# Second half of the adaLN modulation: from matmuls in the first phase to multiply-adds on GpSimd in units 8 to 11

## The chip, the cores and the metric

The kernel runs on one core of a Trainium2 chip. The metric is the device time of one execution in microseconds (us). Three runs of the kernel before took 1102.35, 1103.45 and 1103.99 us; their median is 1103.45 us. Engines are named as in the profile: PE is TensorE's matmul, PEld its weight load, DVE is VectorE, ACT is ScalarE, POOL is GpSimd, and SP is SyncE, which here issues nearly all DMAs. Each engine works through its own instructions in the order written; a wait of one instruction holds everything behind it on that engine.

## The reference

One transformer block over 2048 tokens of width 448, conditioned by a vector `c`: attention with 16 heads of 28, then a GELU MLP of width 1792, each behind a layer norm that is scaled, shifted and gated by six vectors of 448.

```python
mod = (silu(c) @ w_mod).reshape(1, 6, 1, -1)          # c: 1x448, w_mod: 448x2688
sa, ca, ga, sb, cb, gb = (mod[:, i] for i in range(6))
h = layernorm(x) * (1 + ca) + sa
q, k, v = (h @ wqkv) ...                               # 16 heads, 28 each
x = x + ga * (softmax(q @ k.T * 28**-0.5) @ v) @ wo
h = layernorm(x) * (1 + cb) + sb
y = layernorm(h)                                       # the MLP has its own
x = x + gb * (gelu(y @ w1 + b1) @ w2 + b2)
```

All is float32. The change concerns `ga`, `sb`, `cb` and `gb` only: the second part of the modulation, columns 896 to 2687 of `w_mod`.

## The kernel before

Precision is kept by splitting each operand into a high and a low float32 part (`hi`, `lo`), so that a product is three matmuls. The program has three parts in a row.

**The first phase** works on four blocks of 512 tokens. A block `b` is a list of tasks: a Q or K projection for a group of four heads (`qk_task`), or a V projection for 128 tokens (`v_task`). A task is 11 matmuls. The softmax needs the maximum of every score row before the exponentials, and it is found by a cheaper, separate pass: a *row maximum* is one matmul of a 128x28 piece of Q with a 28x512 piece of K (`max_mm`), and a DVE reduction of the 128x512 result to one column (`max_one`). There are 1024 of these, 64 for each *unit* (a group of heads with 512 queries). After each task `emit_task` puts four or five row maxima on PE. Their PSUM banks come from a ring of five (`ps_mx`). A further bank, `o` (`ps_o`), is used for a *sixth* matmul in tasks in which nothing else needs it: the flag `p1_n[1]`. Some tasks also have four row maxima between the halves of their 11 matmuls (`emit_mid`). One matmul in most tasks belongs to a pair: ACT takes the ReLU of a difference and DVE adds the other row maximum (`pair_diff`, its `rest`).

In block 1 the bank `o` is held by the second part of the modulation. Tasks 0 to 3 of that block end with `mod_mm`: four matmuls of 32x448, the SiLU of `c` (32 equal columns) times a piece of `w_mod`, which lies in the slots `v2` and `v3`; so the flag is off for these tasks. `mod_fin` then copies the bank to SBUF on ACT, sends it to DRAM (`drow`) and loads it back four times as a row that every partition holds (`rows["ga"]` and so on).

**The second phase** has 16 units of 16 *steps*, 256 in all. A step does the scores of 128 keys with 512 queries for four heads (12 matmuls, `L1348`), two exponentials on ACT (`L1361`), and the product of the step before with V (`av`, `L1303`). What is left of the row maxima is strewn into the steps. From step 121 (`RING`) there are three a step: one in the only bank `m1`, reduced by `L481`, and two in a double bank of the score tiles, reduced together by `L686`. Steps 8 to 11 of units 13 and 14 also carry the output projection (`is_wo`). When no row maximum is left, the scores take all score tiles (`three`).

At the end of a unit, tasks with fixed steps (`unit_end_tasks`) form the softmax denominators: step 1 of the next unit sends them out over SP (`L1046`), step 4 takes reciprocals on DVE and bounces them through DRAM (`L1054`, `L1056`), step 10 multiplies on POOL (`L1061`), step 11 rounds to `hi` on DVE (`L1071`), takes `lo` on POOL (`L1072`), and stores both. Other work has its step in a table, `sched`, filled by `at(step, fn)`. In each step's list, what was entered first comes first; the entries of the unit ends are made while the program is written out, so they come after those made ahead of it. Steps 4 to 14 hold the preparation of `wo` (scaled by `ga` on POOL, rounded on DVE: `wo_item`), step 15 and 28 the load and scaling of `b2`.

**The third part** is the MLP.

Of the kernel before, what the change touches and what calls it, by code (L numbers as in the profile page):

```python
# [22 lines left out]
D = 448  # L23
# [21 lines left out]
def tile_adaln_block(ctx: ExitStack, tc: tile.TileContext, x, wqkv, wo, w1, b1, w2, b2, c, w_mod, out):  # L45
# [33 lines left out]
    def sbt(tag, shape, dt=F32, bufs=1):  # L79
        return sb.tile(shape, dt, tag=tag, name=nm(tag), bufs=bufs)  # L80
# [40 lines left out]

    ident = sbt("ident", [128, 128])
    make_identity(nc, ident)
    cst = sbt("cst", [128, 5])
    neg_half, zero_col = cst[:, 0:4], cst[:, 4:5]
    pool.memset(neg_half, -0.5)
    pool.memset(zero_col, 0.0)


    cols = sbt("cols", [128, 2 * NC])  # L130
# [607 lines left out]

    mod = {}

    def mod_load(k):
        mod[k] = slot(f"v{2 + k % 2}", [128, 4 * D], F32)
        load_mod(mod[k], k, 2 * D, 4)

    def mod_mm(k):
        if k == 0:
            mod["p"] = ps_o()
        p = mod["p"]
        for j in range(4):
            rs_, cs = mod_part(k, j, 4)  # L750
            pe.matmul(
                p[32 * j : 32 * j + 32, :D], sil_b[rs_, k, :], mod[k][rs_, cs],
                start=(k == 0), stop=(k == NC - 1),
            )

    def mod_fin():
        t = sbt("full", [128, 512], bufs=3)
        act.copy(t[0:64, :D], mod["p"][0:64, :D])
# [58 lines left out]
    for b in range(NB):  # L817
# [12 lines left out]
        for n, (tb, kind, g) in enumerate(tasks):  # L830
# [7 lines left out]
                p1_n[0] = 0  # L838

            k = n - (6, 4, 4, 4)[b]  # L840
            p1_n[1] = not (more and (0 <= k < NC)) and not (b == 1 and n < 4)
            p1_n[2] = (3 if n > 4 else 1) if b == 3 else 2 if b == 2 and p1_n[1] else 1
            p1_n[3] = emit_mid if (b, n) in ((1, 1), (1, 3), (1, 5), (1, 7), (2, 8)) else None
            p1_n[4] = not more
# [27 lines left out]
                    later[n - 7](None)  # L872
            if n == (4 if b else 6):
                v_init(b)
            if b == 0 and n == 6:
                mod_load(0)
                mod_load(1)
# [4 lines left out]
            if b == 1:  # L882
                if n < 2:
                    mod_mm(n)
                    mod_load(2 + n)
                elif n in (2, 3):
                    mod_mm(n)
                    if n == 3:
                        mod_fin()
            if not more:  # L890
                if n == 0:
                    load_q(0)
# [68 lines left out]
    def wo_item(n):  # L961
        def ld(r):
            if n == 4:
                pool.memset(r[:, :D], 0.0)
                for j in range(4):
                    sp.dma_start(r[32 * j : 32 * j + DH, :D], wo[NP + DH * j : NP + DH * j + DH, :])
                return
            p0 = 0
            for r0, r1 in (((128 * n, 128 * n + 128),), MIX_HI, MIX_LO)[max(0, n - 1)]:
                sp.dma_start(r[p0 : p0 + r1 - r0, :D], wo[r0:r1, :])  # L970
                p0 += r1 - r0

        def go(r):
            full = sbt("full", [128, 512], bufs=3)
            ps = slice(0, 112 if n == 3 else 128)
            pool.tensor_tensor(out=full[ps, :D], in0=r[ps, :D], in1=rows["ga"][ps], op=ALU.mult)

            def rest():
                if n == 3:
                    hi = sbt("hi", [128, 512], F32R, bufs=3)  # L980
                    dve.tensor_copy(hi[ps, :D], full[ps, :D])
                    pool.tensor_tensor(out=wo_p[1][ps, 2, :], in0=full[ps, :D], in1=f(hi)[ps, :D], op=ALU.subtract)
                    pool.tensor_copy(wo_p[1][0:32, 2, :], f(hi)[0:32, :D])
                    return
                k = min(n, 3)
                dve.tensor_copy(wo_p[0][:, k, :], full[:, :D])
# [3 lines left out]
            at(6 + 2 * n, rest)  # L990

        return ld, go

# [511 lines left out]
```

## Time and profile before

| | us |
|---|---|
| median of three runs | 1103.45 |
| the profiled execution | 1103.82 |
| its span | 1101.7 |
| first phase (ends with the first score matmul) | 0 to 167.1 |
| second phase, steps 0 to 255 | 167.1 to 791.1 |
| step 121 on, a step without projection | 2.1 to 2.3 |
| last units, no row maximum left | about 2.0 a step |

The times of steps are taken from the first of the twelve score matmuls of each step. A row of the timeline gives the start in us from the span's beginning, the length, the engine, the line, the operation, the tile written and those read, and in brackets the idle time of the engine before it with what ended it. The granted TensorE clock is 1.00 throughout.

### The profile page before, as it was taken

To read this page: it belongs to the slowest core of one execution; us is meant where nothing else is said; L and a number is where in the kernel's file an instruction comes from. 1 tells how busy PE (TensorE), PEld (TensorE's weight loads), DVE (VectorE), ACT (ScalarE), POOL (GpSimd) and SP (SyncE) were. 2 spreads that over 40 slices of the span, in tenths; PEclk is the share of its full clock that TensorE was granted. 3 is DMA by queue.
4 is the path that set the end of the run, shared out by engine and by line. 5 is a ranking of instruction groups with operands and counts; after the bars stand their busy time and mean duration, and the time that the engine had idled before them with its cause. 6 is when DMAs were issued, how large, how long until landed. Compare 5 with 4: busy or idle time off the path is not lost.

```text
span 1101.7 us, 20731 instructions
## 1 busy us (share of the span) xinstructions
PE 1094.3 (99%) x8303; PEld 665.3 (60%) x8303; DVE 798.9 (73%) x1382; ACT 697.3 (63%) x883; POOL 196.8 (18%) x201
## 2 busy tenths in 40 slices
PE   9999999999999999999999999999999999999998
PEld 6756675444444444444444444554488888888887
DVE  6968788999999989988888888574655644444322
ACT  4655667888888888888888888678933411211210
POOL 1543332210000000000000000116123214023000
PEclk9999999999999999999999999999999999999999
DMA  9553354221222201231211313111451000000000
GB/s 311 199 191 106 99 183 138 60 64 33 75 76 61 76 28 40 69 102 47 69 48 38 98 42 99 57 31 59 146 144 50 27 34 1 15 20 1 34 1 34
DMA packets 51094, 82.67 MB, mean 75 GB/s; under 512 B 13327, under 2 KB 19878, under 8 KB 50986
## 3 DMA queue, kind: packets, MB, share of 16 engines
q1 hardware_dynamic: 50514, 80.61, 23.9%
q8 instruction: 65, 1.06, 0.4%
q10 hardware_dynamic: 148, 0.46, 0.1%
q0 software_dynamic: 336, 0.28, 0.1%
q14 instruction: 31, 0.25, 0.1%
HBM read 56.25 MB, written 26.75 MB: 75 GB/s over the span
## 4 chain that ended last, share of the span: by engine, by line
PE 97%; DVE 1%; ACT 0%; DMA 0%; issue 0%; ACTq 0%; DVEq 0%
PE s L1348 23%; PE o L1303 23%; PE m L396 17%; PE pa L396 9%; PE m L476 8%; PE s L1439 3%; PE s L1440 3%; PE s L1438 3%; PE s L476 2%; PE t L1439 1%; PE t L1440 1%; PE t L1438 1%; PE o L277 1%; DVE mxp L481 0%; PE ma L476 0%; PE m L277 0%
## 5 line engine op out<-in xcount | busy, mean ns | idle before, releaser
L481 DVE TENSOR_REDUCE mxp<-m 128x1 f32<-128x512 f32 x555 | 359.9, 686 | 64.7 <-PE m L476 46.9
L1348 PE MATMUL s<-slot_b,slot_a 28*128 28x512 f32 (+1 forms) x3072 | 356.7, 423 | 0.0
L1348 PEld LDWEIGHTS s<-slot_b,slot_a 28*128 28x128 f32 (+1 forms) x3072 | 211.2, 183 | 175.8 <-ACT slot_c L1361 96.4
L476 PE MATMUL m<-kh,qh 28*128 28x512 f32 x607 | 227.0, 468 | 0.4 <-DVE mxp L481 0.3
L1361 ACT ACTIVATE slot_c<-s 128x1024 f32<-128x1024 f32 x170 | 174.8, 1028 | 51.5 <-PE s L1348 50.8
L1303 PE MATMUL o<-slot_c,v 128*32 128x512 f32 x680 | 178.9, 605 | 0.0
L1394 ACT ACTIVATE full<-m,b_col 128x512 f32<-128x512 f32 x56 | 38.6, 689 | 205.3 <-PE m L396 188.5
L686 DVE TENSOR_REDUCE mxp<-s 128x2 f32<-128x1024 f32 x107 | 131.2, 1226 | 5.0
L1303 PE MATMUL o<-slot_c1h,v 128*32 128x512 f32 x512 | 134.7, 605 | 0.0
L1303 PE MATMUL o<-slot_c0h,v 128*32 128x512 f32 x508 | 133.6, 605 | 0.0
L1361 ACT ACTIVATE slot_c1h<-s 128x1024 f32<-128x1024 f32 x128 | 130.7, 1021 | 0.0
L1361 ACT ACTIVATE slot_c0h<-s 128x1024 f32<-128x1024 f32 x127 | 130.5, 1027 | 0.0
L1397 DVE CAST hi<-full 128x512 fp32r<-128x512 f32 x42 | 18.6, 443 | 121.1 <-ACT full L1394 121.1
L1361 ACT ACTIVATE slot_d<-s 128x1024 f32<-128x1024 f32 x86 | 88.4, 1028 | 25.2 <-PE s L1348 24.9
L476 PEld LDWEIGHTS m<-kh,qh 28*128 28x128 f32 x607 | 90.8, 182 | 15.2 <-DVE mxp L481 13.3
L1303 PE MATMUL o<-slot_d,v 128*32 128x512 f32 x344 | 90.5, 605 | 0.4 <-ACT osb L1267 0.4
L1061 POOL TENSOR_TENSOR osb<-osb,osb 128x512 f32<-128x512 f32 x16 | 20.6, 1284 | 363.5 <-DMA osb<-drec 247.1
L1398 DVE TENSOR_TENSOR lo<-full,hi 128x512 fp32r<-128x512 f32 x56 | 43.0, 768 | 26.6 <-ACT hi L1397 22.6
L396 PE MATMUL m<-y,slot_a 128*128 128x512 f32 x160 | 60.7, 395 | 0.0
L481 DVE TENSOR_REDUCE mxp<-ma 128x1 f32<-128x512 f32 x61 | 39.5, 682 | 13.2 <-PE m L476 8.0
L1303 PEld LDWEIGHTS o<-slot_c,v 128*32 128x32 f32 x680 | 24.5, 108 | 39.0 <-issue 36.4
L650 DVE CUSTOM_DVE_ANT_0 slot_d0i<-m,slot_d0i 128x512 f32<-128x512 f32 x54 | 37.3, 691 | 14.3 <-PE m L476 11.6
(351 smaller groups left out, 1835.7 us busy)
## 6 DMA issues: line engine op xcount, KB each, us to landing
slot_b<-d SPq DMA_DIRECT2D x32, 256.0 KB
slot_a<-d SPq DMA_DIRECT2D x32, 256.0 KB
d<-lo SPq DMA_DIRECT2D x28, 256.0 KB
d<-hi SPq DMA_DIRECT2D x16, 256.0 KB
osb<-drec SPq DMA_DIRECT2D x15, 256.0 KB
out_dram<-xn SPq DMA_DIRECT2D x16, 224.0 KB
raw<-in_B_w_dram SPq DMA_DIRECT2D x14, 224.0 KB
qh<-d SPq DMA_DIRECT2D x12, 256.0 KB
```

Source lines behind the costliest of these rows:

```text
L396: pe.matmul(p, a, b, start=(i == 0), stop=(i == len(terms) - 1))
L476: pe.matmul(m, qh_sb[(g, qt)][js, i * 128 : (i + 1) * 128], k[js, :], start=True, stop=True)
L481: dve.tensor_reduce(out=mxp[(g, qt)][:, i, j, cch : cch + 1], in_=m, op=ALU.max, axis=AX.X)
L686: dve.tensor_reduce(out=mxp[(g, qt)][:, i, j : j + 2, cch], in_=t, op=ALU.max, axis=AX.X)
L1303: pe.matmul(o[32 * j : 32 * j + 32, :], v_sb[kt // 4][:, kt % 4, 4 * g + j, :], p[j // 2][:, j % 2, :], start=(kt == 0), stop=(kt == NKT - 1),
L1348: pe.matmul(s2[:, jj, :], ks[rows_, kp, kc], qs[rows_, qp, :], start=(term == 0), stop=(term == 2))
L1361: act.activation(pt[hf], s2, AF.Exp, scale=SCALE)
L1394: act.activation(gf, p, AF.Gelu_apprx_tanh, bias=b1_col[:, i : i + 1])
L1398: dve.tensor_tensor(out=glo, in0=gf, in1=f(ghi), op=ALU.subtract)
L1438: pe.matmul(pp, ghi[:, ts], w_hi, start=(m == 0), stop=False)
L1439: pe.matmul(pp, ghi[:, ts], w_lo, start=False, stop=False)
L1440: pe.matmul(pp, glo[:, ts], w_hi, start=False, stop=(m == NFT - 1))
```

## The change

The second part of the modulation is no longer a matmul. `mod_load` brings a half of a row block of `w_mod` (128x896, 448 KB; the last block has 64 rows) into the one slot `a2h`; `mod_add` multiplies it on POOL by the SiLU column of `c` and adds it to a running sum in `b1h` (for `ga`, `sb`) or `a3h` (for `cb`, `gb`). There are eight such pairs of load and multiply-add, one every three steps from step 130 (`MOD_AT`): the load at steps 130, 133, ... 151, the multiply-add two steps after each. At step 156 `mod_fin` sums over the partitions with four matmuls against a column of ones, in a bank of `ps_mx`, and goes on as before, with one ACT copy for three.

The preparation of `wo`, which needs `ga`, moves from steps 0 to 14 to steps 162 to 176 (`WO_AT`), and that of `b2` from 15 and 28 to 177 and 190. A second SiLU of `c` without the 32 copies is taken at the start (`sil_c`), and one more memset fills the bias column `third`. In tasks 0 to 3 of block 1 the flag for the sixth matmul is now set.

```diff
+MOD_AT = 130
+WO_AT = 166
...
+    act.activation(sil_c, pc[:, :NC], AF.Silu)
...
-    def mod_load(k):
-        mod[k] = slot(f"v{2 + k % 2}", [128, 4 * D], F32)
-        load_mod(mod[k], k, 2 * D, 4)
-
-    def mod_mm(k):
...
+    def mod_load(h, k):
+        rs_ = mod_rows(h, k)
+        mod["raw"] = slot("a2h", [128, 2 * D], F32)
+        c0 = 2 * D * (1 + h)
+        sp.dma_start(mod["raw"][rs_], w_mod[128 * k : min(128 * k + 128, D), c0 : c0 + 2 * D])
+
+    def mod_add(h, k):
+        rs_ = mod_rows(h, k)
+        if k == 0:
+            mod[h] = slot(("b1h", "a3h")[h], [128, 2 * D], F32)
+        raw, total = mod["raw"][rs_], mod[h][rs_]
+        col = sil_c[rs_, k : k + 1].broadcast_to([rs_.stop - rs_.start, 2 * D])
+        pool.tensor_tensor(out=raw if k else total, in0=raw, in1=col, op=ALU.mult)
+        if k:
+            pool.tensor_tensor(out=total, in0=total, in1=raw, op=ALU.add)
+
+    def mod_fin():
+        p = ps_mx()
+        ones_ = v_sb[0].rearrange("p t h d -> p (t h) d")[:, 0:32, DH]
         for j in range(4):
             pe.matmul(
-                p[32 * j : 32 * j + 32, :D], sil_b[rs_, k, :], mod[k][rs_, cs],
-                start=(k == 0), stop=(k == NC - 1),
+                p[32 * j : 32 * j + 32, :D], ones_, mod[j // 2][:, j % 2 * D : (j % 2 + 1) * D], start=True, stop=True,
             )
-
-    def mod_fin():
         t = sbt("full", [128, 512], bufs=3)
-        act.copy(t[0:64, :D], mod["p"][0:64, :D])
-        act.activation(t[64:96, :D], mod["p"][64:96, :D], AF.Identity, bias=1.0)
-        act.copy(t[96:128, :D], mod["p"][96:128, :D])
+        act.activation(t[:, :D], p[:, :D], AF.Identity, bias=third)
...
-            p1_n[1] = not (more and (0 <= k < NC)) and not (b == 1 and n < 4)
+            p1_n[1] = not (more and (0 <= k < NC))
...
-    at(0, lambda: wo_prep.load(2))
+    for i in range(2 * NC):
+        h, k = divmod(i, NC)
+        at(MOD_AT + 3 * i, lambda h=h, k=k: mod_load(h, k))
+        at(MOD_AT + 3 * i + 2, lambda h=h, k=k: mod_add(h, k))
+    at(MOD_AT + 6 * NC + 2, mod_fin)
+    at(WO_AT - 4, lambda: wo_prep.load(2))
     for n in range(5):
-        at(4 + 2 * n, wo_prep.step)
+        at(WO_AT + 2 * n, wo_prep.step)
...
-    at(15, b2_load)
-    at(28, b2_mul)
+    at(WO_AT + 11, b2_load)
+    at(WO_AT + 24, b2_mul)
```

Line numbers from the middle of the program on grow by 2 to 7: the row maximum's matmul `L476` is `L481` after, the unit end's `L1061`, `L1071`, `L1072` are `L1063`, `L1073`, `L1074`, the scores `L1348` are `L1355`.

Three places show how the order of instructions moves. The first is PE in the first phase, block 1, the end of task 3: `ma`, `m` and `o` are PSUM banks, `raw` a tile with the difference of two K pieces or a K piece, `kh` and `osb` others. Before:

```order
L476 MATMUL m_203_899<-raw_734,qh_158_707 128x512
L476 MATMUL ma_902<-kh_162_729,qh_60_322 128x512
L476 MATMUL ma_905<-kh_162_729,qh_60_322 128x512
L476 MATMUL m_206_908<-kh_74_360,qh_158_707 128x512
L751 MATMUL o_760<-slot_v_187_822,slot_d_4_86 32x448 x4
L396 MATMUL pa_941<-slot_c_110_509,slot_a_18_123 128x512
```

After:

```order
L481 MATMUL ma_886<-raw_733,qh_157_706 128x512
L481 MATMUL ma_889<-raw_806,osb_340 128x512
L481 MATMUL m_203_892<-kh_161_728,qh_61_325 128x512
L481 MATMUL m_204_895<-raw_806,osb_340 128x512
L481 MATMUL m_205_898<-kh_75_363,qh_157_706 128x512
L401 MATMUL pa_914<-slot_c_111_512,slot_a_19_125 128x512
```

The four modulation matmuls are gone and one row-maximum matmul is added. Task 1 goes from four to five in the same way and task 2 from five to six; task 0 has none before or after. So the first phase has 207 row-maximum matmuls where it had 204, and the second 817 where it had 820.

The second place is POOL around the end of unit 7 (steps 128 to 140); `osb` is the unit's output, `slot_a2h` the loaded piece of `w_mod`. Before:

```order
L517 MEMSET m_1700_6922 128x16
L1061 TENSOR_TENSOR osb_6951<-osb_6813,osb_6951 128x512
L1072 TENSOR_TENSOR lo_7160<-osb_6951,hi_7159 128x512
L517 MEMSET m_1838_7554 128x16
L1061 TENSOR_TENSOR osb_7453<-osb_7316,osb_7453 128x512
```

After:

```order
L522 MEMSET m_1664_6774 128x16
L761 TENSOR_TENSOR slot_b1h_6886<-slot_a2h_6826,sil_c_86 128x896
L761 TENSOR_TENSOR slot_a2h_6922<-slot_a2h_6922,sil_c_86 128x896
L763 TENSOR_TENSOR slot_b1h_6886<-slot_b1h_6886,slot_a2h_6922 128x896
L761 TENSOR_TENSOR slot_a2h_7013<-slot_a2h_7013,sil_c_86 128x896
L763 TENSOR_TENSOR slot_b1h_6886<-slot_b1h_6886,slot_a2h_7013 128x896
L1063 TENSOR_TENSOR osb_6891<-osb_6749,osb_6891 128x512
L1074 TENSOR_TENSOR lo_7110<-osb_6891,hi_7109 128x512
L761 TENSOR_TENSOR slot_a2h_7107<-slot_a2h_7107,sil_c_86 64x896
```

Five new instructions on three loaded pieces now stand ahead of the unit end's multiplication. On DVE the rounding that reads its result keeps its place between two reductions (`mxp` is the tile of maxima):

```order
L691 TENSOR_REDUCE mxp_6618<-s_1735_7096 128x2
L1073 CAST hi_7109<-osb_6891 128x512
L486 TENSOR_REDUCE mxp_6618<-m_1742_7126 128x1
L691 TENSOR_REDUCE mxp_6618<-s_1744_7139 128x2
```

The third place is SP at the same steps; `den` and `drec` are denominators and reciprocals, `slot_b` a unit's Q with the row maxima written into it (`L533`). Before:

```order
L528 DMA slot_b_1682_6847<-full_6850 4x4x32 x4
L508 DMA qh_1701_6925<-d_236 128x512
L1054 DMA drec_6949<-den_6845 128x16
L1056 DMA osb_6951<-drec_6949 128x1x512
L508 DMA kh_1736_7091<-d_244 128x512
L1082 DMA o_2029<-hi_7159 28x512 x4
```

After:

```order
L533 DMA slot_b_1667_6788<-full_6791 4x4x32 x4
L753 DMA slot_a2h_6826<-in_w_mod_dram 128x896
L1056 DMA drec_6889<-den_6786 128x16
L1058 DMA osb_6891<-drec_6889 128x1x512
L753 DMA slot_a2h_6922<-in_w_mod_dram 128x896
L753 DMA slot_a2h_7013<-in_w_mod_dram 128x896
L513 DMA kh_1723_7037<-d_247 128x512
L753 DMA slot_a2h_7107<-in_w_mod_dram 64x896
L1084 DMA o_2002<-hi_7109 28x512 x4
```

The first load stands behind the row maxima's DMAs of unit 9, the second behind those of the reciprocals. Since there is one slot, each load from the second on waits for POOL to have read the piece before it.

More of the change, by code (lines that the diff above doesn't have):

```diff
@@ L123, in tile_adaln_block @@
     make_identity(nc, ident)
-    cst = sbt("cst", [128, 5])
-    neg_half, zero_col = cst[:, 0:4], cst[:, 4:5]
+    cst = sbt("cst", [128, 6])
+    neg_half, zero_col, third = cst[:, 0:4], cst[:, 4:5], cst[:, 5:6]
     pool.memset(neg_half, -0.5)
-    pool.memset(zero_col, 0.0)
+    pool.memset(cst[:, 4:6], 0.0)
+    pool.memset(third[64:96], 1.0)
+    sil_c = sbt("sil_c", [128, NC])
     cols = sbt("cols", [128, 2 * NC])
@@ L739, in tile_adaln_block, with mod_rows @@
     mod = {}
[L741 to L748 removed]
+    def mod_rows(h, k):
+        return slice(0, 128) if k < 3 else slice(64 * h, 64 * h + 64)
+    def mod_load(h, k):
[5 more added lines that the diff above has]
+        rs_ = mod_rows(h, k)
+        if k == 0:
+            mod[h] = slot(("b1h", "a3h")[h], [128, 2 * D], F32)
[7 more added lines that the diff above has]
+        ones_ = v_sb[0].rearrange("p t h d -> p (t h) d")[:, 0:32, DH]
         for j in range(4):
[L750 removed]
             pe.matmul(
[L752 to L753 removed]
+                p[32 * j : 32 * j + 32, :D], ones_, mod[j // 2][:, j % 2 * D : (j % 2 + 1) * D], start=True, stop=True,
             )
[L756 removed]
         t = sbt("full", [128, 512], bufs=3)
[L758 to L760 removed]
+        act.activation(t[:, :D], p[:, :D], AF.Identity, bias=third)
         sp.dma_start(drow, t[0:128:32, :D])
@@ L874, in tile_adaln_block @@
                 v_init(b)
-            if b == 0 and n == 6:
-                mod_load(0)
-                mod_load(1)
             if b == 1 and n == 8:
@@ L881, in tile_adaln_block @@
                 sp.dma_start(b1_col, b1.rearrange("(k p) -> p k", p=128))
[L882 to L889, printed above, removed]
             if not more:
@@ L988, in rest @@
                     pool.tensor_tensor(out=wo_p[1][:, k, :], in0=full[:, :D], in1=f(wo_p[0])[:, k, :], op=ALU.subtract)
-            at(6 + 2 * n, rest)
+            at(WO_AT + 2 + 2 * n, rest)
         return ld, go
```

## The prediction

> **What bounds the kernel now.** I read the page's busy times and chain first, then windows of the stages that the change touches, then the timeline around them.
>
> ```profile
> PE 1094.3 (99%) x8303; PEld 665.3 (60%) x8303; DVE 798.9 (73%) x1382; ACT 697.3 (63%) x883; POOL 196.8 (18%) x201
> PE 97%; DVE 1%; ACT 0%; DMA 0%; issue 0%; ACTq 0%; DVEq 0%
> 58.34:76.56 18.22, 18.22 (x98) 9.83 (x98) 11.07 (x21) 11.15 (x22) 5.46 (x6) 1.00 0.65 209
> 505.97:523.85 17.88, 17.88 (x189) 7.69 (x186) 15.61 (x18) 15.41 (x17) 2.63 (x3) 1.00 0.16 41
> ```
>
> The chain of work that ended last lies 97% on PE: time taken off PE's queue shortens the kernel, if PE then does not wait. The windows' columns are length, then busy PE, PEld, DVE, ACT, POOL. In the first (the four tasks that lose the modulation matmuls) DVE is busy 61% of the time, so it has room. In the second (steps 136 to 143, within the stretch that takes the new POOL work) DVE is busy 87% and POOL 15%: DVE has little room, POOL much. What matters is who waits for POOL.
>
> **First phase: what is freed and what takes it back.** These are matmuls and reductions of block 1, tasks 0 to 3.
>
> ```profile
> 58.34 0.96 PE L751 MATMUL o<-slot_v,slot_d 128*32 128x448 f32 x8
> 59.23 1.20 PE L396 MATMUL pa<-slot_c,slot_a 128*128 128x512 f32 x4
> 60.58 0.51 PE L476 MATMUL m<-kh,qh 28*128 28x512 f32 x3
> 62.62 0.93 PE L476 MATMUL m<-kh,qh 28*128 28x512 f32 x3
> 63.48 0.96 PE L751 MATMUL o<-slot_v,slot_d 128*32 128x448 f32 x8
> 64.37 1.21 PE L396 MATMUL pa<-slot_c,slot_a 128*128 128x512 f32 x4
> 67.14 0.72 PE L476 MATMUL m<-kh,qh 28*128 28x512 f32 x3
> 67.79 0.96 PE L751 MATMUL o<-slot_v,slot_d 128*32 128x448 f32 x8
> ...
> 61.12 1.89 DVE L481 TENSOR_REDUCE mxp<-m 128x1 f32<-128x512 f32 x3 [5.10 <-PE ma L476]
> 62.92 0.68 DVE L481 TENSOR_REDUCE mxp<-ma 128x1 f32<-128x512 f32 x1
> ```
>
> A set of modulation matmuls holds PE 0.89 us (58.34 to 59.23; 63.48 to 64.37 again), so four give 3.56. A row maximum costs PE 0 to 0.22: sets of five take 0.66 (67.13 to 67.79), a sixth runs beside the fifth. But each costs DVE 0.63 (three in 1.89), and the modulation matmuls were also the time in which DVE emptied banks. I count forward from 58.34, with five ring banks, DVE starting 0.54 after the first matmul, 0.63 a reduction, and 0.42 from the last row-maximum matmul to the next task. Task 1 starts at 58.34 instead of 59.23; its inner four at 59.69; DVE ends them at 60.87, 61.49, 62.12 and 62.70. Its closing set, at 61.72, has five matmuls; the fifth needs the last of those banks, so it goes at 62.75 and task 2 starts at 63.17 (before: 64.37). Task 2 finds its banks empty: 2.77 of projection, 0.66 of maxima, so task 3 starts at 66.60. There the fourth inner matmul waits for a reduction to 68.48, and its closing set has nine reductions ahead of it: they end at 72.35, and task 4 starts at 72.82 (before: 73.82). So 1.0 of the 3.56 arrives. The ends are 3.1 (3.56 less twice 0.22, DVE hidden) and 0.5 (another 0.5 of bank waits); I take 1.0, since a reckoned wait of 0.45 in task 1 before (62.61 to 63.06) is what the trace shows. By task 4 DVE is idle again, so the gain carries on to the end of the phase. The second SiLU, one memset and the absent `w_mod` loads lie beside other work: 0, at most 0.3 either way.
>
> **The wait in step 140.** This is the main term. The rows are the DMA queue, POOL, DVE and PE at the end of unit 7.
>
> ```profile
> 491.36 0.60 SPq L1046 DMA_DIRECT2D den<-osb  x1
> 492.00 0.95 SPq L774 DMA_DIRECT2D slot_b<-d  x2
> 495.51 2.27 SPq L528 DMA_DIRECT2D slot_b<-full  x4
> 501.41 0.56 SPq L1056 DMA_DIRECT2D osb<-drec  x1
> ...
> 506.65 1.29 POOL L1061 TENSOR_TENSOR osb<-osb,osb 128x512 f32<-128x512 f32 x1 [25.65 <-ACT slot_c1h L1361]
> 515.58 1.29 POOL L1072 TENSOR_TENSOR lo<-osb,hi 128x512 fp32r<-128x512 f32 x1 [7.64 <-DVE hi L1071]
> ...
> 515.09 0.42 DVE L1071 CAST hi<-osb 128x512 fp32r<-128x512 f32 x1
> 515.55 0.69 DVE L481 TENSOR_REDUCE mxp<-m 128x1 f32<-128x512 f32 x1
> 516.22 1.23 DVE L686 TENSOR_REDUCE mxp<-s 128x2 f32<-128x1024 f32 x1
> 517.12 0.18 PEld L1348 LDWEIGHTS s<-slot_b,slot_a 29*128 29x128 f32 x2 [0.84 <-ACT slot_c L1361]
> 517.46 0.77 PE L1348 MATMUL s<-slot_b,slot_a 28*128 28x512 f32 x8
> 517.70 0.69 DVE L481 TENSOR_REDUCE mxp<-m 128x1 f32<-128x512 f32 x1 [0.25 <-PE s L1348]
> ```
>
> Before, POOL multiplies at 506.65, as soon as the reciprocals have landed, 8.4 us ahead of the rounding (`L1071`) that DVE reaches at 515.09. After, five POOL instructions and three loads in series stand in front of it, with one slot. A POOL instruction on 896 elements is not in the trace; its size follows from two smaller ones:
>
> ```profile
> L1061 POOL TENSOR_TENSOR osb<-osb,osb 128x512 f32<-128x512 f32 x16 | 20.6, 1284 | 363.5 <-DMA osb<-drec 247.1 <-ACT slot_c1h L1361 51.3 <-ACT slot_c L1361 35.1
> L1123 POOL TENSOR_TENSOR xn<-xn,row_cb 128x448 f32<-128x448 f32 x16 | 18.6, 1161 | 38.4 <-PE s L1440 24.2 <-DVE xn L217 12.5 <-PE m L396 1.7
> ```
>
> 64 elements more cost 123 ns, so 896 cost 1161 + 448 x 1.92 = 2021 ns: 2.0 us (bounds 1.8 and 2.3). A load of 448 KB: the two 256 KB loads issued from 492.00 have landed by 495.51, when `L528` goes on writing the same tile, so 3.5 us for 512 KB. I take 3.5 for the single 448 KB one too; 3.1 is the low end (by size alone), 4.2 the high one, since the second load meets the 256 KB of reciprocals, which need 501.41 to 506.65.
>
> SP is free for the first load at 495.51 + 2.27 = 497.8. From there load, multiply (2.0), load, multiply and add (4.0), load, multiply and add (4.0), then the unit end's 1.3: 497.8 + 3 x 3.5 + 10.0 + 1.3 = 519.6. DVE wants the result at 515.1 and waits 4.5. Behind it in DVE's queue stand both kinds of reductions: the single bank `m1` is wanted by PE at 517.12, and the scores of step 141 (517.46) need the tile whose reduction ended at 516.22 + 1.23 = 517.45. That is no slack but DVE's 0.25 of idle time, so PE loses 4.3. With the bounds, 497.8 + 9.3 + 9.0 + 1.3 = 517.4 gives 2.3 and 497.8 + 12.6 + 11.5 + 1.3 = 523.2 gives 8.1.
>
> [...]
>
> The five remaining pieces come later: the shift of 4.5 gives them time, and counted on in the same way POOL reaches the multiplication of unit 8's end about 1 us before DVE's rounding at step 156 (551.15 before) and the last sum 3 us before `mod_fin`. So no second wait; at the slow bounds one of up to 2. SP's other DMAs behind waiting loads (denominators, K pieces) have several steps until use.
>
> **`mod_fin` in step 156.** Four matmuls of the shape of `L751`: 0.89 on PE. They take `m1`, which the next step wants at once, and it is free only when ACT has copied it.
>
> ```profile
> 74.55 0.51 ACT L758 COPY full<-o 64x448 f32<-64x448 f32 x1
> 516.90 1.02 ACT L1361 ACTIVATE slot_c0h<-s 128x1024 f32<-128x1024 f32 x1
> ```
>
> The copy starts when the last matmul ends (0.96 after the first, and 0.1 on), about when the exponential ahead of it has ended too (517.92, 0.8 after the step's start), and takes 0.54. PE waits for it some 0.8. Together 1.7; bounds 0.9 (wait hidden) and 2.2.
>
> **What leaves the second phase.** It has three row-maximum matmuls less: one more in step 81 (+0.1), and steps 233 and 234 have two and none instead of three each. These rows are the first score matmuls of steps 233 to 236.
>
> ```profile
> 735.83 0.50 PE L1348 MATMUL s<-slot_b,slot_a 29*128 29x512 f32 x2
> 740.61 0.50 PE L1348 MATMUL s<-slot_b,slot_a 29*128 29x512 f32 x2
> 745.40 0.99 PE L1348 MATMUL s<-slot_b,slot_a 29*128 29x512 f32 x12
> 749.75 0.99 PE L1348 MATMUL s<-slot_b,slot_a 29*128 29x512 f32 x12
> ```
>
> Step 234 took 4.79 with three, step 235 took 4.35 with none: -0.44, and -0.1 for step 233. In sum -0.4.
>
> **The moved preparation of `wo`.** Five roundings leave the first steps, where they hid, for steps 168 to 176:
>
> ```profile
> L986 DVE CAST slot_e<-full x4: 382/383/384, 186.7 to 206.8; 128x448 fp32r<-128x448 f32 x4
> ```
>
> 0.38 each, less than the rounding of 0.42 after which DVE still had 0.25 idle in the step shown, so 0; without that cover 5 x 0.38 = 1.9. POOL is idle there and the four rows have some ten steps to arrive.
>
> **Sum.** -1.0 + 4.3 + 1.7 - 0.4 = +4.6 us. The profiled execution took 1103.82 us, so 1108.4 by it; against the median of the runs, 1103.45, which is 0.4 lower, 1108.1. I say 1108.2. What can be told from no change is 0.2%, about 2.2 us.
>
> **Rivals.**
> - *POOL keeps up.* If a POOL instruction takes 1.3 whatever its width and a load 3.1, the result is there at 497.8 + 9.3 + 6.5 + 1.3 = 514.9, before DVE wants it. Then -1.0 + 1.7 - 0.4 leaves +0.3: 1103.8, no change. For it: the idle POOL (15%). Against it: 512 elements already take 1284 ns.
> - *The freed matmuls arrive in full.* With POOL keeping up, and DVE's reductions hidden in the first phase, -3.1 + 0.9 - 0.4 = -2.6: 1100.9, faster. It is decided by whether five banks bridge the reductions of tasks 1 and 3; the wait of 0.45 that is there already speaks against it.
> - *The chain of loads falls behind for good.* With 4.2 a load and 2.3 an instruction the first wait is 8.1, unit 8's end waits too (2), and the roundings show: 1103.5 - 1.0 + 8.1 + 2 + 1.7 - 0.4 + 0.5 = 1114.4.
> - *The sixth maximum doesn't come as named*: only three tasks get one more, since task 0 has no row maximum to give. This is in the sum already.
>
> **Chances and range.** Forecast with its bounds 0.70, POOL keeping up 0.11, faster 0.06, falling behind 0.13. The range holds the forecast with the lower and upper ends of wait and first phase together, 1105.0 (wait 2.3, gain 2.0) to 1112.5 (wait 8.1, gain 1.0, `mod_fin` 2.2). Faster by over 0.2%: 0.06. Within 0.2%: 0.13, with a little of the forecast's lower edge. Slower by over 0.2%: 0.81.
>
> **What would show it.** In the profile after: an idle time of DVE of some 4 us before `L1073` near step 140, released by POOL, and a gap of PE there; POOL's `L761` and `L763` at 2.0 us; none of it before the second `L1073`. Task 4 of block 1 about 1 us earlier, not 3. A PE wait after `mod_fin`'s matmuls ended by ACT. The forecast falls if the first multiplication of the unit end (`L1063`) is done before DVE gets there, or if a second wait stands at step 156.

## The result and the profile after

| us | before | after |
|---|---|---|
| median, runs beside each other | 1103.61 (4 runs, 1102.35 to 1103.99) | 1112.03 (4 runs, 1111.54 to 1113.95) |
| the profiled execution | 1103.82 | 1113.95 |
| its span | 1101.7 | 1112.2 |

The ratio of the runs is 1.0082, with a 95% interval of 1.0066 to 1.0098 (the two medians alone give 1.0076). The kernel is slower, as forecast, but by 8.4 us and not by 4.6. The profiled execution is the longest of the four; the others had spans of 1109.7 to 1110.6 us.

These are the busy times and the chain of work that ended last, of the kernel after.

```profile
PE 1097.6 (99%) x8279; PEld 666.3 (60%) x8279; DVE 797.1 (72%) x1382; ACT 697.2 (63%) x883; POOL 222.3 (20%) x216
PE 92%; DVE 3%; DMA 2%; POOL 1%; ACT 1%; issue 0%; SPq 0%; DVEq 0%; POOLq 0%; ACTq 0%
```

The chain was 97% PE and is 92%: DVE, a DMA and POOL are on it now. PE's busy time is 3.3 us *longer* although 24 matmuls are gone, so some matmuls must have become slower. The next rows are SP, POOL, DVE and PE of the kernel after, around step 140.

```profile
498.08 0.44 SPq L753 DMA_DIRECT2D slot_a2h<-in_w_mod_dram  x1
501.70 0.55 SPq L1058 DMA_DIRECT2D osb<-drec  x1
503.31 9.50 SPq L753 DMA_DIRECT2D slot_a2h<-in_w_mod_dram  x2
...
501.60 1.68 POOL L761 TENSOR_TENSOR slot_b1h<-slot_a2h,sil_c 128x896 f32<-128x896 f32 x1 [21.02 <-DMA slot_a2h<-in_w_mod_dram]
508.59 1.68 POOL L761 TENSOR_TENSOR slot_a2h<-slot_a2h,sil_c 128x896 f32<-128x896 f32 x1 [5.31 <-DMA slot_a2h<-in_w_mod_dram]
510.35 2.10 POOL L763 TENSOR_TENSOR slot_b1h<-slot_b1h,slot_a2h 128x896 f32<-128x896 f32 x1
516.03 1.68 POOL L761 TENSOR_TENSOR slot_a2h<-slot_a2h,sil_c 128x896 f32<-128x896 f32 x1 [3.58 <-DMA slot_a2h<-in_w_mod_dram]
...
519.82 1.26 POOL L1063 TENSOR_TENSOR osb<-osb,osb 128x512 f32<-128x512 f32 x1
...
521.11 0.43 DVE L1073 CAST hi<-osb 128x512 fp32r<-128x512 f32 x1 [6.29 <-POOL osb L1063]
...
522.19 0.79 PE L481 MATMUL m<-kh,qh 28*128 28x512 f32 x1 [4.92 <-DVE mxp L486]
...
524.90 1.07 PE L1310 MATMUL o<-slot_c,v 128*32 128x512 f32 x2
```

The forecast chain is there: load, multiply, load, multiply and add, load, multiply and add, and only then the unit end's product (`L1063`). The first load took 3.5 us (498.08 to 501.60), the second 5.3 (503.31 to 508.59), the third 3.55. DVE waited 6.29 us for the product, PE 4.92 for DVE. Then look at the two PE rows: a matmul of `L481` with 28x512 takes 0.79 where it takes 0.50 elsewhere, and those of `L1310` take 1.06 each, where the same ones in the kernel before (`L1303`) take 0.605 on average. The windows of the same stretch say why; the column behind POOL is the granted clock.

```profile
515.00:520.00 5.00, 2.27 (x25) 0.71 (x20) 0.00 (x0) 2.13 (x3) 3.89 (x3) 1.00 0.19 71
520.00:525.00 5.00, 2.81 (x17) 1.43 (x21) 3.15 (x5) 1.02 (x1) 4.02 (x3) 0.54 0.47 117
525.00:530.00 5.00, 5.00 (x31) 1.52 (x31) 2.63 (x3) 2.56 (x3) 2.07 (x1) 0.50 0.40 111
530.00:535.00 5.00, 5.00 (x50) 1.86 (x46) 3.51 (x5) 3.55 (x5) 1.68 (x1) 0.93 0.36 80
```

After PE has stood still (3.15 us of the 4.92 by then), its clock is granted at one half, from 520.42 to 530.66 by the trace's record of the clock (so 0.54 and 0.93 in the windows that are cut). That is 10.24 us; in 8.5 of them (from 522.19 on) PE is busy at half its clock. Step 141 takes 10.00 us where it took 2.30, step 142 takes 3.87 where it took 2.27: 9.3 us in all.

The second place is unit 8's end and `mod_fin`, rows of POOL and DVE after:

```profile
557.21 1.28 POOL L1063 TENSOR_TENSOR osb<-osb,osb 128x512 f32<-128x512 f32 x1
...
560.05 0.42 DVE L1073 CAST hi<-osb 128x512 fp32r<-128x512 f32 x1
...
564.19 0.69 DVE L486 TENSOR_REDUCE mxp<-m 128x1 f32<-128x512 f32 x1 [1.92 <-PE m L481]
```

The product ends at 558.49, 1.56 before DVE's rounding: no second wait here. The 1.92 of idle DVE belong to `mod_fin`; steps 156 and 157 take 0.76 and 0.78 longer, and the two steps behind them 0.11 less.

Steps of the two profiled executions, measured by their first score matmul, add up so:

| | us |
|---|---|
| start of the first phase, before the changed tasks | +0.8 |
| first phase from there | -1.7 |
| steps 0 to 127 | +0.6 |
| steps 141 and 142 | +9.3 |
| steps 156 to 159 (`mod_fin`) | +1.4 |
| steps 160 to 191 (`wo`, `b2`) | +0.45 |
| the rest of the second phase | +0.1 |
| third part | -0.4 |
| sum | +10.5 |

The first line is not put down to the change. A second stretch of half clock in the start-up is on record in the kernel after (8.43 to 11.84) and in one of the kernels below, whose start-up is that of the kernel before (11.23 to 14.64; it is 1.5 us late); among the others the start of block 1 lies between 0.2 us later and 1.35 us earlier than before. In the kernel before, too, the record of the clock says 1.00 only from 10.60 on, and not throughout: the first transposes on PE take 0.42 us each, the same ones behind that point 0.28.

### The profile page after: what moved, and what is told of

Its sections match the earlier page's. It is cut to its first block, busy times and chain, and to the rows that moved or that the text cites. A ratio compares the mean times of both kernels' runs of the same rounds, so it can differ in the third digit from the quotient of the medians.

```text
span 1112.2 us, 20702 instructions
## 1 busy us (share of the span) xinstructions
PE 1097.6 (99%) x8279; PEld 666.3 (60%) x8279; DVE 797.1 (72%) x1382; ACT 697.2 (63%) x883; POOL 222.3 (20%) x216
## 3 DMA queue, kind: packets, MB, share of 16 engines
q8 instruction: 65, 1.06, 0.4%
## 4 chain that ended last, share of the span: by engine, by line
PE 92%; DVE 3%; DMA 2%; POOL 1%; ACT 1%; issue 0%; SPq 0%; DVEq 0%; POOLq 0%; ACTq 0%
PE s L1355 22%; PE o L1310 22%; PE m L401 17%; PE pa L401 8%; PE m L481 7%; PE s L1446 3%; PE s L1447 3%; PE s L1445 3%; DVE mxp L486 2%; PE s L481 1%; PE ma L481 1%; DMA slot_a2h<-in_w_mod_dram 1%; PE t L1446 1%; PE t L1447 1%; PE t L1445 1%; DMA slot_c0h<-in_w_mod_dram 1%
## 5 line engine op out<-in xcount | busy, mean ns | idle before, releaser
L486 DVE TENSOR_REDUCE mxp<-m 128x1 f32<-128x512 f32 x581 | 374.9, 685 | 71.2 <-PE m L481 61.1
L1355 PE MATMUL s<-slot_b,slot_a 28*128 28x512 f32 (+1 forms) x3072 | 360.5, 426 | 0.0
L1355 PEld LDWEIGHTS s<-slot_b,slot_a 28*128 28x128 f32 (+1 forms) x3072 | 213.1, 184 | 176.9 <-ACT slot_c L1368 96.4
L481 PE MATMUL m<-kh,qh 28*128 28x512 f32 x613 | 225.2, 471 | 5.6 <-DVE mxp L486 4.9
L1310 PE MATMUL o<-slot_c,v 128*32 128x512 f32 x680 | 179.7, 607 | 0.0
L1310 PE MATMUL o<-slot_c1h,v 128*32 128x512 f32 x512 | 135.5, 608 | 0.0
L1310 PE MATMUL o<-slot_c0h,v 128*32 128x512 f32 x508 | 134.5, 608 | 0.0
L481 PEld LDWEIGHTS m<-kh,qh 28*128 28x128 f32 x613 | 89.9, 182 | 22.1 <-DVE mxp L486 19.6
L1310 PE MATMUL o<-slot_d,v 128*32 128x512 f32 x344 | 91.3, 610 | 0.4 <-ACT osb L1274 0.4
L1063 POOL TENSOR_TENSOR osb<-osb,osb 128x512 f32<-128x512 f32 x16 | 20.5, 1282 | 308.3 <-DMA osb<-drec 295.6
L481 PE MATMUL s<-kh,qh 28*128 28x512 f32 x214 | 48.2, 443 | 0.0
L1310 PEld LDWEIGHTS o<-slot_c,v 128*32 128x32 f32 x680 | 24.5, 108 | 39.6 <-issue 37.3
```

The source lines that it names most:

```text
L481: pe.matmul(m, qh_sb[(g, qt)][js, i * 128 : (i + 1) * 128], k[js, :], start=True, stop=True)
L486: dve.tensor_reduce(out=mxp[(g, qt)][:, i, j, cch : cch + 1], in_=m, op=ALU.max, axis=AX.X)
L1310: pe.matmul(o[32 * j : 32 * j + 32, :], v_sb[kt // 4][:, kt % 4, 4 * g + j, :], p[j // 2][:, j % 2, :], start=(kt == 0), stop=(kt == NKT - 1),
L1355: pe.matmul(s2[:, jj, :], ks[rows_, kp, kc], qs[rows_, qp, :], start=(term == 0), stop=(term == 2))
```

## The experiments

**1. Was it the wait itself, or the clock behind it?** The kernel after, with six zero matmuls added into the running `o` between steps 140 and 141, so that PE has work while DVE waits.

```diff
+                if step == 140:
+                    zeros_ = v_sb[0].rearrange("p t h d -> p (t h) d")[:, 0:32, DH + 1]
+                    for _ in range(FILL):
+                        pe.matmul(po[0:32, :D], zeros_, acc[3][:, 0, :], start=False, stop=False)
```

> The changed kernel with six more matmuls (zeros times a piece of x, added to the running output, about 0.76 us each) on PE between steps 140 and 141, where PE stands idle for 4.9 us. The wait for POOL stays. Theory (about 4 us of the loss is PE's clock after the idle stretch): the granted clock stays at 1.00 through steps 141 to 144, and although PE has 4.6 us more to do the kernel is 2 to 4 us faster than the changed one: 1108 to 1110. Rival (the time after the wait is DVE's backlog, and the half clock only goes with it): same time as the changed kernel or more, 1112 to 1114.

Measured: 1110.19 us, 1.0063 (1.0048 to 1.0078), 1.8 us less than after and 0.2 above what was expected. The intervals of the two kernels overlap, so it is the profiles that tell them apart. DVE still waited, 5.91 us, but the windows show a full clock:

```profile
515.00:520.00 5.00, 5.00 (x22) 1.57 (x13) 0.63 (x2) 1.08 (x2) 4.38 (x4) 1.00 0.10 22
520.00:525.00 5.00, 4.55 (x42) 1.93 (x46) 4.32 (x6) 2.59 (x3) 4.57 (x3) 1.00 0.42 116
```

Steps 128 to 142 took 5.6 longer than before instead of 9.3. So the wait is worth 5.6, and the half clock 3.7 in the profiled execution (up to 0.4 less, since DVE's wait is 0.4 shorter here). Among the four executions of the kernel after, those with a mean granted clock of 0.997 had spans of 1109.7 and 1109.9, the one at 0.995 had 1110.6 and the profiled one, at 0.993, 1112.2: the half clock, that of the start-up included, lasts for a different time in each.

**2. The wait alone, in the kernel before.** Nothing of the change, only extra POOL multiplications of 128x512 ahead of unit 7's product; ten, eight and seven of them.

```diff
+            if u == 7:
+                scratch = slot("a2h", [128, 512], F32)
+                for _ in range(10):
+                    pool.tensor_tensor(out=scratch, in0=o_sb, in1=st["rb"], op=ALU.mult)
```

> As the one with eight, but ten: DVE's wait becomes 5.7 us, PE's idle stretch 4.3. Theory (an idle stretch of PE of between 1.7 and 4.3 us brings the half clock): PE loses 5.3 us for the wait and 2 to 4.5 more for a clock of 0.5 over 7 to 10 us: 1110.5 to 1113, so the last two POOL instructions cost 5 to 7 us for 2.6 us of POOL. Rival (the wait alone): 1109.

> The kernel before with eight extra POOL multiplications of 1.28 us on the landed reciprocals ahead of the one at unit 7's end, and nothing else. POOL then delivers at about 518.2 what DVE wants at 515.1: a wait of 3.1 us, and PE idle for 1.7. Theory: PE loses 2.5 to 3 us and the clock stays at 1.00: 1106 to 1106.7. Rival (every such wait costs about 1.5 times its length): 1108 or more. Rival (a wait on DVE is hidden by PE's banks): 1103.6.

> The kernel before with seven more multiplications of 128x512 on POOL ahead of unit 7's product (eight gave a wait of DVE of 3.3 us, a gap of PE of 1.9 and half clock for 3.4 us; ten gave 5.8, 4.5 and 10.2). One fewer takes 1.3 us off the wait: DVE waits 2.0, PE 0.6 to 0.7. Theory: PE's clock falls only where it stands still for more than a us or so within one stretch of 3.4 us; here it stays at 1.00, and steps 141 and 142 take 2 to 2.7 longer: 1105.5 (1104.5 to 1106.5). Rival: every wait of this kind halves the clock for a stretch, and the loss is 3.5 or more: 1107 or more.

Measured: 1111.02 us with ten (1.0069, 1.0054 to 1.0084), 1109.18 with eight (1.0046, 1.0030 to 1.0063), 1105.08 with seven (1.0027, 1.0015 to 1.0038). The rows are the rounding of DVE, the first PE matmul behind the gap, and windows; first ten multiplications:

```profile
520.84 0.43 DVE L1075 CAST hi<-osb 128x512 fp32r<-128x512 f32 x1 [5.83 <-POOL osb L1065]
...
521.92 0.79 PE L476 MATMUL m<-kh,qh 28*128 28x512 f32 x1 [4.46 <-DVE mxp L481]
...
520.00:525.00 5.00, 3.08 (x17) 1.53 (x21) 3.42 (x5) 1.22 (x2) 2.13 (x3) 0.50 0.33 82
```

Eight:

```profile
520.01 0.43 DVE L1075 CAST hi<-osb 128x512 fp32r<-128x512 f32 x1 [3.30 <-POOL osb L1065]
...
521.09 0.50 PE L476 MATMUL m<-kh,qh 28*128 28x512 f32 x1 [1.93 <-DVE mxp L481]
...
520.00:525.00 5.00, 3.51 (x25) 1.01 (x25) 3.98 (x5) 2.05 (x2) 1.32 (x2) 0.82 0.37 92
525.00:530.00 5.00, 5.00 (x46) 2.28 (x46) 3.47 (x4) 3.11 (x4) 0.00 (x0) 0.84 0.00 0
```

Seven:

```profile
516.81 0.43 DVE L1075 CAST hi<-osb 128x512 fp32r<-128x512 f32 x1 [2.02 <-POOL osb L1065]
...
517.89 0.50 PE L476 MATMUL m<-kh,qh 28*128 28x512 f32 x1 [0.65 <-DVE mxp L481]
...
515.00:520.00 5.00, 3.96 (x42) 1.55 (x41) 2.94 (x5) 3.21 (x4) 3.03 (x4) 1.00 0.23 56
```

| kernel | DVE waits | longest PE gap | half clock for | steps 141 and 142 |
|---|---|---|---|---|
| before, seven | 2.02 | 0.65 | 0 | +1.7 |
| before, eight | 3.30 | 1.93 | 3.41 | +4.6 |
| before, ten | 5.83 | 4.46 | 10.24 | +8.3 |
| after | 6.29 | 4.92 | 10.24 | +9.3 |

The expectation for eight missed: I held a gap of 1.9 us to be too short for the clock. It isn't; one multiplication more than seven cost 2.9 us in the profiles where it takes 1.3. (In the profiled execution of eight the start-up also lost 1.5 us, as in the table of the result; this adds to its time, not to its steps.) Ten came out as expected, and seven within its range: up to there the wait costs about its own length (1.7 for 2.02) and no more. A wait of the length of the kernel after's, put into the kernel before, costs nearly the kernel after's loss; nothing else in the change is needed to explain steps 141 and 142.

**3. Does the order on POOL cause the wait?** The kernel after, with the third multiply-add behind the product of unit 7's end, the eighth behind that of unit 8's, and `mod_fin` two steps later.

```diff
-        at(MOD_AT + 3 * i + 2, lambda h=h, k=k: mod_add(h, k))
-    at(MOD_AT + 6 * NC + 2, mod_fin)
+        at(MOD_AT + 3 * i + 2 + {2: 1, 7: 2}.get(i, 0), lambda h=h, k=k: mod_add(h, k))
+    at(MOD_AT + 6 * NC + 4, mod_fin)
```

> The changed kernel with three entries of its table one or two steps later: the multiply-add of the third piece at step 139 and of the eighth at 155, so that on POOL the unit end's multiplication stands ahead of both, and the sum over partitions at 158. All the work stays. Theory (DVE waits in step 141 for POOL's queue, and PE, left idle, then runs at half clock): the wait of 6.3 us before the rounding goes, the granted clock stays at 1.00 in the second phase, steps 141 and 142 take 4.6 us together instead of 13.9, and the kernel takes 1103 to 1104.5. Rival (the POOL and DMA work itself slows the other engines, wherever it stands): it stays at 1110 or more, with the loss spread over steps 130 to 156.

Measured: 1111.95 us, 1.0074 (1.0059 to 1.0089). The expectation missed: the wait of step 140 is gone, but the time came back in step 154 (+5.8, and 0.6 each in steps 150 and 155). These are rows of DVE (step 140, no wait), POOL, SP and PE in this kernel:

```profile
513.41 0.42 DVE L1073 CAST hi<-osb 128x512 fp32r<-128x512 f32 x1
...
529.59 1.68 POOL L761 TENSOR_TENSOR slot_a3h<-slot_a2h,sil_c 128x896 f32<-128x896 f32 x1 [3.38 <-DMA slot_a2h<-in_w_mod_dram]
...
531.30 0.33 SPq L753 DMA_DIRECT2D slot_a2h<-in_w_mod_dram  x1
531.73 0.60 SPq L1048 DMA_DIRECT2D den<-osb  x1
...
544.04 0.43 SPq L513 DMA_DIRECT2D kh<-d  x1
...
549.25 0.76 PE L481 MATMUL m<-kh,qh 28*128 28x512 f32 x1 [3.58 <-DMA kh<-d]
```

SP issues the load at 531.30, 0.03 after POOL has freed the one slot (529.59 + 1.68 = 531.27), and unit 8's denominators only behind it. Everything in SP's queue is late from there, among it a K piece (issued at 544.04) for which PE waits 3.58 us; the clock is at one half for 6.83 us from 548.06 on. So a wait of a load for its slot holds all of SP's queue, which I had passed over with "several steps until use".

**4. Take the loads off SP's queue, or give the pairs more steps.** The first kernel is that of experiment 3 with the eight loads issued by GpSimd. The second is the kernel after with a pair every four steps for every three, on SP's queue as before; `mod_fin` is in step 164, `WO_AT` is 174.

```diff
-        sp.dma_start(mod["raw"][rs_], w_mod[...])
+        pool.dma_start(mod["raw"][rs_], w_mod[...])
```

> The kernel with the unit ends ahead of the multiply-adds, in which the stall had moved to step 154, but with the eight loads issued by GpSimd in place of SyncE. Theory: the stall in step 154 came because a load that waits for the slot held SyncE's queue and with it the K piece behind; without the loads in that queue the K piece comes in time, and the stall of 5.8 us and the half clock after it go: 1104 (1102.5 to 1106). Rival: the DMA engines themselves were late (too many bytes at once), or GpSimd is late in any case: the stall stays in step 154 or comes back at a unit end, 1108 or more.

```diff
-WO_AT = 166
+WO_AT = 174
...
-        at(MOD_AT + 3 * i, lambda h=h, k=k: mod_load(h, k))
-        at(MOD_AT + 3 * i + 2, lambda h=h, k=k: mod_add(h, k))
-    at(MOD_AT + 6 * NC + 2, mod_fin)
+        at(MOD_AT + 4 * i, lambda h=h, k=k: mod_load(h, k))
+        at(MOD_AT + 4 * i + 2, lambda h=h, k=k: mod_add(h, k))
+    at(MOD_AT + 8 * NC + 2, mod_fin)
```

> The changed kernel with one pair of load and multiply-add every four steps for three (mod_fin in step 164, the preparation of wo and b2 eight steps later). Theory: the eight us are lost because a load of 3.5 us and four us of POOL, in series through one slot, don't fit three steps of 2.3 us; in four steps (9.2 us) they do, so neither POOL is late for the unit ends in steps 140 and 156 nor does a waiting load hold SP. Then no PE gap over 1 us in steps 128 to 166, the granted clock stays at 1.00, and the sum is that of the rest: first phase -2.3 to -1.7, steps 80 to 96 +0.45, mod_fin +1.5, the end +0.2: 1103.5 (1102.5 to 1105.5). Rival: GpSimd and the loads beside the second phase cost by themselves (contention, or one of the two queues is still late): 1107 or more, with a stall near step 140 or 156.

Measured: 1103.04 us (0.9999, 0.9990 to 1.0009) and 1103.24 us (1.0003, 0.9993 to 1.0013). Both are level with the kernel before; neither has a stall near steps 140 or 156, and the clock is 1.00 from the start-up on. With a pair every four steps SP sends the denominators of unit 8 at 525.59 and the K piece at 536.18, 6 and 8 us earlier than in experiment 3, and POOL is done with the product before DVE comes:

```profile
525.59 0.60 SPq L1048 DMA_DIRECT2D den<-osb  x1
...
536.18 0.43 SPq L513 DMA_DIRECT2D kh<-d  x1
...
510.81 1.29 POOL L1063 TENSOR_TENSOR osb<-osb,osb 128x512 f32<-128x512 f32 x1
...
515.15 1.68 POOL L761 TENSOR_TENSOR slot_a2h<-slot_a2h,sil_c 128x896 f32<-128x896 f32 x1
...
513.41 0.42 DVE L1073 CAST hi<-osb 128x512 fp32r<-128x512 f32 x1
```

The last POOL row is the third multiply-add. At four steps a pair it is entered in step 140, behind the product of step 138, so this kernel changes the order on POOL as experiment 3 does; what the spacing adds is that the loads hold SP's queue for less time.

In this kernel steps 128 to 163, in which all eight loads and multiply-adds lie, take 0.1 us less than before. So the modulation's second part costs the second phase no contention to speak of: the eight us lie in the two queues.

**5. Only the queue.** The kernel after with that one word changed, and its own order of the multiply-adds.

> The changed kernel with one word changed: the eight loads are issued by GpSimd in place of SyncE; order and steps of the multiply-adds stay. Theory: in the changed kernel POOL was late in step 140 because SyncE, which issues in program order and first waits for the pieces of step 128, reaches the first load only at 498; GpSimd is idle from 480 on and starts there, so three pieces are done some ten us earlier and the rounding finds its product: no PE gap over 1 us in step 140, no half clock, first phase -1.65, drift +0.45, mod_fin +1.5, end +0.2: 1103.2 (1102.3 to 1105). Rival: the order is what matters, since the third multiply-add ahead of the unit end's product makes POOL late whatever queue issues: a wait of 2 us or more in step 140 and 1107 or more.

Measured: 1103.86 us (1.0008, 0.9999 to 1.0017). POOL and DVE in this kernel:

```profile
478.56 0.78 POOL L753 DMA_DIRECT2D slot_a2h<-in_w_mod_dram  x1
...
503.80 1.28 POOL L1063 TENSOR_TENSOR osb<-osb,osb 128x512 f32<-128x512 f32 x1 [1.81 <-DMA osb<-drec]
...
550.57 0.43 DVE L1073 CAST hi<-osb 128x512 fp32r<-128x512 f32 x1 [1.81 <-POOL osb L1063]
```

GpSimd starts the first load at 478.56, not at 498.08, and with the same order the product waits for the reciprocals alone. So the wait of step 140 needs two things together: the third multiply-add ahead of the product, and a first load that SP reaches only at 498. Either one changed alone takes the wait away, the order in experiment 3 and the start of the loads here. What is left is a wait of 1.81 at unit 8's end: PE is not held back in step 140 any more, so it comes to step 156 earlier than POOL.

**6. What is the sixth row maximum worth?** The kernel after without that part: the flag stays off in tasks 0 to 3 of block 1.

```diff
-            p1_n[1] = not (more and (0 <= k < NC))
+            p1_n[1] = not (more and (0 <= k < NC)) and not (b == 1 and n < 4)
```

> The changed kernel without its second part: the flag for the sixth row maximum stays off in tasks 0 to 3 of block 1, so the three row maxima return to the second phase. Theory: the freed matmuls arrive nearly in full when no maximum is added (first phase -2.5 to -3.2 where it is -1.75 to -2.3), the drift of +0.45 in steps 80 to 96 and the slower step 235 go; the loss near step 140 (9.3) and mod_fin (1.5) stay: 1111.2 (1110 to 1112.5), at most 1 us faster than the changed kernel. Rival, as the prediction had it: the maxima returned to the second phase cost it 0.4 and the first phase gains no more than 1.0 to 1.5: 1112.5 or more.

Measured: 1110.84 us (1.0072, 1.0057 to 1.0087). The rows are the first matmul of tasks 0 and 4 of block 1: before,

```profile
49.94 0.50 PE L396 MATMUL pa<-slot_c,slot_a 128*128 128x512 f32 x1
...
73.82 0.50 PE L396 MATMUL pa<-slot_c,slot_a 128*128 128x512 f32 x1
```

after,

```profile
50.71 0.50 PE L401 MATMUL pa<-slot_c,slot_a 128*128 128x512 f32 x1
...
72.99 0.50 PE L401 MATMUL pa<-slot_c,slot_a 128*128 128x512 f32 x1
```

and without the sixth.

```profile
49.52 0.50 PE L401 MATMUL pa<-slot_c,slot_a 128*128 128x512 f32 x1
...
69.99 0.49 PE L401 MATMUL pa<-slot_c,slot_a 128*128 128x512 f32 x1
```

The four tasks take 23.88, 22.28 and 20.47 us. Of the 3.56 that the modulation matmuls held, 3.4 arrive when no maximum is added, and 1.6 with the three. Each added maximum costs 0.6 there on average. That is about a DVE reduction (0.63), but that DVE sets it is not shown: PE stands idle for 0.9 of the 1.8, and the longest of these waits, in task 2, is ended by ACT, which frees the bank of a pair.

```profile
67.63 0.49 PE L481 MATMUL ma<-kh,qh 28*128 28x512 f32 x1 [0.68 <-ACT slot_d0h L494]
```

This wait stands in every kernel here with the sixth, and in none without it. In the second phase the three moved maxima save nothing: the drift in steps 0 to 127 is +0.1 without them (+0.6 with them), and the end of the row maxima compares so. First score matmuls of steps 235 and 236, after:

```profile
755.61 1.66 PE L1355 MATMUL s<-slot_b,slot_a 29*128 29x512 f32 x12
760.62 0.99 PE L1355 MATMUL s<-slot_b,slot_a 29*128 29x512 f32 x12
```

Without the sixth:

```profile
753.21 0.99 PE L1355 MATMUL s<-slot_b,slot_a 29*128 29x512 f32 x12
757.56 0.99 PE L1355 MATMUL s<-slot_b,slot_a 29*128 29x512 f32 x12
```

Step 235 takes 5.01 with the three moved maxima and 4.35 without, as before; every kernel here with the sixth shows this, none without it. It gives back the 0.21 and 0.44 that steps 233 and 234 save. Why the first score matmuls after the last maximum take longer there is not settled. In all the second part of the change loses about 2.3 us (1.8 in the first phase, 0.5 in steps 0 to 127). Without it the kernel gained only 1.2 of them: in its profile PE comes to step 156 earlier by 3.9 us than in the kernel after (1.2 of them from the start-up), POOL's product of unit 8 ends only 0.7 earlier, and DVE waits for it, so that step 156 takes 1.83 longer than before and not 0.76:

```profile
557.85 0.43 DVE L1073 CAST hi<-osb 128x512 fp32r<-128x512 f32 x1 [1.65 <-POOL osb L1063]
```

The first wait is still there in this kernel. PE's gap behind it is longer than in the kernel after, 5.31 us for 4.92, yet the half clock lasts 6.83 us (from 518.57 on) and not 10.24:

```profile
519.17 0.79 PE L481 MATMUL m<-kh,qh 28*128 28x512 f32 x1 [5.31 <-DVE mxp L486]
```

**7. The parts together.** A pair every four steps, no sixth maximum, and `mod_fin` ahead of the product with V in step 164.

```diff
+            if step == MOD_AT + 8 * NC + 2:
+                mod_fin()
             if pend is not None:
                 pu, pkt, pp, po = pend
                 av(pu, pkt, pp, po)
```

> The kernel with a pair every four steps, without the sixth row maxima, and with mod_fin at the start of step 164 for its end, so that the copy on ScalarE stands ahead of that step's exponentials. Theory: the parts add up: first phase -2.5 to -3.2, no drift, mod_fin 0.9 to 1.5, nothing else: 1102 (1101 to 1103.5), which would be level with the kernel before or up to 0.2% ahead. Rival: mod_fin's bank is waited for as before or longer, and the first phase gives less: 1104 or more.

Measured: 1101.10 us (10 runs, 1100.47 to 1101.99) against 1103.02 before: 0.9984 (0.9975 to 0.9993), a little faster than before. The edit put `mod_fin` behind the scores of its step and not at its start as the expectation says, so ScalarE's copy still stood behind two exponentials; steps 164 and 165 lost 1.2 us where the second kernel of experiment 4 lost 1.4.

## Why the prediction came out as it did

- **The bound and the place: right.** PE's queue is the bound, and the loss is at the product of unit 7's end, by the chain that the prediction counted from SP's row at 498.
- **The wait of DVE: 6.29 us for 4.5.** POOL was slightly faster than reckoned (1.68 for a multiplication by a column, 2.10 for an addition; 9.2 us in sum for 10.0). The second load took 5.3 us, beyond the upper end of 4.2. In the kernel after and the one with a pair every four steps, the three loads issued some 1.6 us behind the 256 KB of reciprocals took 5.0 to 5.5 us, the others on SP's queue 3.3 to 3.6, but for one of 4.5 (532.33 to 536.80 in the kernel after). So the term was seen (the prediction named this meeting) and sized too small; that this sharing is the reason was not tried alone. The low end of 3.1 for 448 KB was not reached either: 3.3 at least from SP's queue, and 3.8 in the median of the six that GpSimd issued in experiment 4.
- **"PE loses 4.3": the step that failed.** PE lost 9.3 in the profile. About 5.6 are the wait, 3.7 the half clock behind it (experiment 1), for which the prediction has no term: it reckons PE at full clock after the wait and gives no reason. The kernel before could not show otherwise, since PE's longest idle time in its whole second phase is 0.42 us. That 1112.03 still lies inside the range is luck: the upper end of 1112.5 is made of a wait of 8.1, and the wait was 6.29.
- **"So no second wait": right for the kernel after, by a margin of 1.56** (1 us was reckoned), because PE was 9 us late itself. Where PE comes to step 156 earlier, a second of 1.81 or 1.65 stands there (experiments 5 and 6).
- **"SP's other DMAs behind waiting loads have several steps until use": true for the kernel after, and too easy.** In experiment 3 one of them cost 7 us.
- **`mod_fin`: right.** 1.4 for 1.7.
- **First phase: 1.6 for 1.0, near by luck.** From the start of task 1 to that of task 4 the bank count gave 14.5 us, and 14.0 were taken. But it gave task 3 6.2 us where it took 4.9, and task 2 3.4 where it took 4.35, with the wait for ACT that the count leaves out. Its sense, that the added maxima take back much of what the matmuls free, is what experiment 6 shows: 0.6 each, not PE's 0 to 0.22. The window that it read DVE's room from is not that of the four tasks, which run from 49.94 to 73.82; in these DVE is busy 67% of the time and not 61%.
- **What leaves the second phase: 0 for -0.4 at its end, and +0.6 in steps 0 to 127 for +0.1.** Step 234 saved 0.44 as counted and step 233 0.21; that step 235 gives them back was not foreseen, nor the drift, 0.4 of which lies in steps 80 to 95.
- **`wo` and `b2`: +0.45 for 0**, inside the bound of 1.9.
- **The rivals.** That POOL keeps up did not come true here. It does once the loads start earlier or lie further apart, and the time it gave, 1103.8, is near what those kernels took (1103.04 to 1103.86), though their first phase, `wo` and drift are not those of its sum. The rival of a chain that falls behind for good (1114.4) came nearest in the cost of the first wait (8.1), by another mechanism.

## What to carry to other kernels

A wait that lets PE stand still cost its length here and then, from a gap of somewhere between one and two us on (0.96 brought none, 1.93 brought 3.41 us), a stretch at half clock: count both, or give PE something to do. Work that is moved to an idle engine comes with its loads, and the queue that issues them decides when it starts (the first load went out at 498.08 from SyncE's queue and at 478.56 from GpSimd's) and who is held by a full buffer (in experiment 3 PE waited 3.58 us for a K piece issued late): look at the queue ahead of the engine. A row maximum for which PE's rows show 0 to 0.22 us cost 0.6 in a stage where others must first empty its bank: count the engines behind the matmul too.

## What the runs showed of the hardware

The half clock lasted 3.41, 6.83 or 10.24 us, always a multiple of 3.41. It came after PE gaps of 1.93, 3.58, 4.46, 4.92 and 5.31 us, not after one of 0.96 (experiment 5) and not after gaps of 0.65 and 0.40 close together. The longest gap brought 6.83 and that of 4.46 brought 10.24, so the length of the gap alone does not set it.

In the kernel after, the record of the clock changes at 8.43, 11.84, 520.42 and 530.66 us; from the second to the third are 508.6 us, 149 times 3.413. If the time of a kernel is laid out in stretches of 3.413 us from such a change, PE's idle time in them compares so. With ten extra multiplications the half clock began behind a stretch in which PE was idle for 1.57 us, with eight behind one with 1.68. Without the sixth maximum a stretch with 1.30 was followed by a full clock. If the idle time in such a stretch decides, the limit lies between 1.30 and 1.57 us here; this is an estimate from these three kernels, and no run was made to try it. The "more than a us or so within one stretch of 3.4 us" in the expectation for seven was an estimate of the author's too.

A waiting instruction held what stood behind it: the reduction behind DVE's rounding of step 140 had its matmul done at 515.00 in the kernel after (514.51 + 0.49) and started at 521.46, when the wait of 6.29 us was over; for SP's queue the rows of experiment 3 show it.

GpSimd took 1.68 us for a multiplication of 128x896 by a column and 2.10 for an addition of two such tiles, and with 64 rows the same (1.67 and 2.07 at 523.31 and 525.06 in the kernel after).
